# Top-k attention and two MLPs on one core: round one with 256 tokens in two halves, e scaled on GpSimd in the last two rounds, and another order

## The chip, the core and the metric

The kernel runs on one core of one Trainium2 chip. The engines are called by their profile names: PE (TensorE, the matmuls; PEld its weight loads), DVE (VectorE), ACT (ScalarE), POOL (GpSimd) and SP (SyncE, whose queue issues nearly all DMAs). The metric is the device time of one execution in microseconds. Inputs and outputs lie in device memory; working tiles lie in SBUF and matmul results in PSUM.

## What is computed

Attention over 2 batches of 8 heads, 576 positions, head size 64, in which each row keeps its 32 largest scores; its output, 1152 tokens of 512 numbers, goes through two MLPs with a hidden size of 2048.

```python
scores = scale * np.matmul(q, k.transpose(0, 1, 3, 2))
kth = np.partition(scores, -top_k, axis=-1)[..., -top_k:-top_k + 1]   # top_k = 32
scores = np.where(scores >= kth, scores, -1000000000.0)
attn = np.exp(scores - max); attn = attn / (sum + 1e-09)
x = matmul(attn, v) as (1152, 512)
h = x @ w_in;  g = h * np.tanh(softplus(h));  x = g @ w_out        # first MLP (mish)
h = x @ w_in2; g = np.maximum(h, 0) ** 2;     out = g @ w_out2     # second MLP (squared relu)
```

The weights reach the kernel as 64-bit floating-point numbers, seen as pairs of 32-bit words.

## The kernel before

**Rounds.** `ROUNDS` cuts the 1152 tokens into four rounds of 192, 320, 320 and 320 tokens. The code counts them from 0; in this text "round one" is round 0 of the code. While the MLPs of a round run on PE, the attention of the next rounds runs between their matmuls.

**Attention.** A round works through groups of tokens and, for each, four pairs of heads. A *tile* is 128 rows of scores against 576 keys (`tile_of`; a remainder of 64 tokens makes one tile of two heads); all rounds together have 72. A tile's steps: scores on PE into PSUM (line 411); copy to `s` by ACT; the 32nd largest on DVE by four MAX8 (427, 431) and three MATCH_REPLACE8 (430) that write `w`; `nm` on POOL (441); two ACT passes that make `e`; five transposes of `e` on PE (452, 454); copy to `pt` by ACT. `pair_end` waits for all tiles of a pair of heads and multiplies `pt` with the values (497). `inverse` takes the sums of `e`, adds 1e-9 (482, POOL), inverts them (527, DVE), spreads them over partitions with matmuls against the identity (534, 537) and copies them to `inv` by ACT; the product is scaled by `inv` on DVE into `x1` (512).

**MLPs.** Each round has four phases of 64 products of 128x128 weights: `in_phase`, `out_phase`, and both again for the second MLP (all in line 741). Round one uses 32-bit matmuls, two instructions each. The other rounds split weights and activations into a high and a low part and use three matmuls per product. `in_phase` needs `x1` of all four pairs of heads before it gets past its first output tile. Splitting `x` (276), `g` (276, POOL) and squaring (936 POOL, 938 DVE in the last round, `RELU`) lie on the other engines.

**Weights.** The weights are 32 pieces of 128x1024. `convert` makes each into 32-bit numbers in round one: 1 MB read, one ACT pass, one POOL pass (636), one DVE pass (638). Pieces 0 to 23 are then split (`split_w`: high part on ACT, low part in four instructions on POOL, 287) and stored to device memory; the last eight are stored unsplit and split in round two (`fetch_late`). Rounds two to four fetch the split pieces again. A converted piece waits in a place of its own until the phase that uses it releases it: four places used `once` (free parts of `first` and `stage`, and `xl`) and six halves of three shared buffers that come back when their piece has been used.

**Order.** `Order` is a planner: every step is a process that asks for an engine with a cost and a rank; the lowest rank goes first, and the instructions are written to each engine's queue in that order. On the chip each queue runs strictly in this order and waits by semaphores. The numbers at the head (`BUFS`, `CONV_EVERY`, `EARLY`, `STAY`, ...) and the ranks steer it.

## Time and profile before

| | us |
|---|---|
| median of 3 runs | 685.98 (684.62 to 689.83) |
| the profiled execution | 684.57 |
| its span, first to last instruction | 682.8 |

The span is what the views cut into stretches; the profiled execution is 1.8 us longer than its span and 0.2% below the median. Over the span PE is busy for 89%, DVE for 68%, ACT for 59% and POOL for 52%. Such averages hide that the kernel has stages: PE waits in the first hundred microseconds and has the engines nearly to itself in the last two hundred. Matmuls overlap, so that "busy" PE can still run below its rate; the distance between the starts of matmuls tells the rate.

### The profile page before, as it was taken

How to read it: one execution, taken by the hardware profiler on the slowest of the kernel's cores; microseconds unless marked ns; L12 is line 12 of the kernel's file. 1: busy time of each engine (PE TensorE's matmuls, PEld its weight loads, DVE VectorE, ACT ScalarE, POOL GpSimd, SP SyncE). 2: the span in 40 equal slices, each digit the busy share in tenths (PEclk: the TensorE clock that was granted, in tenths of full speed). 3: DMA queues.
4: the chain of work that ended last, by engine and by line, in shares of the span. 5: the costliest groups of instructions: out<-in, count | busy, mean ns of one | idle time of the engine just before them, and what ended most of it. 6: DMA issues, size and time to landing. Idle time of an engine off the chain costs nothing.

```text
span 682.8 us, 11207 instructions
## 1 busy us (share of the span) xinstructions
PE 608.7 (89%) x4104; PEld 559.7 (82%) x4104; DVE 464.1 (68%) x832; ACT 406.0 (59%) x723; POOL 356.2 (52%) x478
## 2 busy tenths in 40 slices
PE   4456569998969799979999999999999999999998
PEld 3334349987767678968889988898999999999997
DVE  5979999999888999988999999997500100001410
ACT  3656568977785567994668877599704404502410
POOL 7998662597996565760238886023207703501420
PEclk9976679999989999999999999999999999999999
DMA  9688851499869989964563379885668899888870
GB/s 345 224 332 311 323 207 75 142 379 381 308 256 369 417 329 394 417 243 148 219 206 111 144 249 347 357 314 198 232 235 304 298 308 325 301 304 304 304 257 29
DMA packets 36598, 186.84 MB, mean 274 GB/s; under 512 B 5312, under 2 KB 11456, under 8 KB 17088
## 3 DMA queue, kind: packets, MB, share of 16 engines
q1 hardware_dynamic: 36272, 185.94, 73.5%
q8 instruction: 32, 0.52, 0.3%
q10 hardware_dynamic: 272, 0.20, 0.1%
q14 instruction: 22, 0.18, 0.1%
HBM read 146.01 MB, written 40.11 MB: 273 GB/s over the span
## 4 chain that ended last, share of the span: by engine, by line
PE 58%; DVE 22%; POOL 11%; ACT 3%; issue 3%; DMA 3%; DVEq 0%; POOLq 0%; ACTq 0%
PE pm L741 48%; DVE w L430 8%; DVE mx L431 7%; POOL w L287 4%; DVE w L638 4%; PE ps L411 3%; PE px L497 3%; DVE mx L427 2%; PE pt L452 2%; POOL stage L636 2%; POOL gl L276 1%; DMA stage<-in_weights 1%; ACT w L270 1%; POOL nm L441 1%; DMA w<-kept 1%
## 5 line engine op out<-in xcount | busy, mean ns | idle before, releaser
L741 PE MATMUL pm<-xh,w 128*128 128x320 f32 (+1 forms) x896 | 200.2, 315 | 5.5 <-ACT xh L270 2.8
L741 PE MATMUL pm<-gh,w 128*128 128x320 f32 x768 | 177.8, 313 | 0.0
L431 DVE MAX8 mx<-w 128x8 f32<-128x576 f32 x216 | 164.4, 761 | 7.4
L741 PEld LDWEIGHTS pm<-xh,w 128*128 128x128 f32 x896 | 152.7, 191 | 7.2 <-ACT xh L270 3.1
L741 PEld LDWEIGHTS pm<-gh,w 128*128 128x128 f32 x768 | 131.0, 189 | 0.7 <-issue 0.3
L741 PE MATMUL pm<-gl,w 128*128 128x320 f32 x384 | 119.7, 312 | 2.2 <-POOL gl L276 2.2
L741 PE MATMUL pm<-xl,w 128*128 128x320 f32 x384 | 119.1, 310 | 0.0
L430 DVE MATCH_REPLACE8 w<-mx,w 128x576 f32<-128x576 f32 x144 | 106.9, 742 | 0.0
L276 POOL TENSOR_TENSOR gl<-h,gh 128x320 fp32r<-128x320 f32 x64 | 56.2, 884 | 85.0 <-ACT gh L270 84.0
L287 POOL TENSOR_TENSOR w<-w,w 128x256 fp32r<-128x256 f32 x112 | 82.8, 763 | 23.3 <-ACT w L270 19.0
L452 PE MATMUL pt<-ident,e 128*128 128x128 f32 x288 | 50.1, 302 | 39.3 <-ACT e L270 36.6
L441 POOL TENSOR_SCALAR nm<-mx 128x1 f32<-128x1 f32 x72 | 31.8, 441 | 85.4 <-DVE mx L431 74.1
L452 PEld LDWEIGHTS pt<-ident,e 128*128 128x128 f32 x288 | 37.6, 153 | 46.4 <-ACT e L270 42.0
L741 PEld LDWEIGHTS pm<-gl,w 128*128 128x128 f32 x384 | 72.8, 190 | 3.0 <-POOL gl L276 2.9
L741 PEld LDWEIGHTS pm<-xl,w 128*128 128x128 f32 x384 | 72.2, 188 | 0.0
L276 DVE TENSOR_TENSOR xl<-pm,xh 128x320 fp32r<-128x320 f32 x12 | 5.9, 488 | 96.8 <-ACT xh L270 96.7
L270 ACT ACTIVATE pt<-pt 128x640 f32<-128x640 f32 x72 | 50.5, 702 | 31.6 <-PE pt L454 31.3
L270 ACT ACTIVATE e<-e,nm 128x576 f32<-128x576 f32 x72 | 55.7, 773 | 19.3 <-POOL nm L441 15.2
L427 DVE MAX8 mx<-s 128x8 f32<-128x576 f32 x72 | 53.5, 743 | 15.9 <-ACT s L270 15.9
L270 ACT ACTIVATE e<-s,mx 128x576 f32<-128x576 f32 x72 | 55.0, 770 | 15.4 <-DVE mx L431 15.2
L430 DVE MATCH_REPLACE8 w<-mx,s 128x576 f32<-128x576 f32 x72 | 53.5, 743 | 0.0
L270 ACT ACTIVATE s<-ps 128x576 f32<-128x576 f32 x72 | 45.8, 636 | 12.2 <-PE ps L411 12.2
(96 smaller groups left out, 988.0 us busy)
## 6 DMA issues: line engine op xcount, KB each, us to landing
w<-both SPq DMA_DIRECT2D x88, 1024.0 KB, 4.9
both<-w SPq DMA_DIRECT2D x32, 1024.0 KB, 6.7
stage<-in_weights SPq DMA_DIRECT2D x22, 1024.0 KB, 7.1
w<-in_weights SPq DMA_DIRECT2D x10, 1024.0 KB, 7.0
vt<-in_v SPq DMA_DIRECT2D x20, 320.0 KB, 4.6
kr<-in_k SPq DMA_DIRECT2D x8, 576.0 KB, 7.6
kept<-w SPq DMA_DIRECT2D x8, 512.0 KB, 11.9
w<-kept SPq DMA_DIRECT2D x8, 512.0 KB, 4.0
```

What stands on the lines that cost most here:

```text
L270: op = ("ACT", t, rank, lambda: nc.scalar.activation(out, in_, func, **kw))
L276: return ({"g": "POOL", "v": "DVE"}[e], t, rank, lambda: eng.tensor_tensor(out=out, in0=in0, in1=in1, op=ALU.subtract))
L287: yield ("POOL", 0.1 + 0.0026 * n, rank, lambda: nc.gpsimd.tensor_tensor(out=out[:, z], in0=in0[:, z], in1=in1[:, z], op=op))
L411: nc.tensor.matmul(sp[:, i, 0:HK], q_, k_[:, i * HK:(i + 1) * HK], start=l == 0, stop=l == len(steps) - 1)
L427: nc.vector.max(out=mx[:, 0, :], in_=s)
L430: nc.vector.match_replace(out=w, in_to_replace=mx[:, i - 1, :], in_values=s if i == 1 else w, imm_value=LOWEST)
L431: nc.vector.max(out=mx[:, i, :], in_=w)
L441: yield ("POOL", 0.38, 1, lambda: nc.gpsimd.tensor_scalar(out=nm, in0=thr, scalar1=mx[:, 0, 0:1], scalar2=scale / UP, op0=ALU.subtract, op ...
L452: nc.tensor.transpose(pp[:, c * P:(c + 1) * P], e[:, c * P:(c + 1) * P], ident)
L497: nc.tensor.matmul(xo[a * D:(a + 1) * D, 0:n], vt[z, a, c, :], pt[z, a, c, 0:n], start=c == 0, stop=c == NK)
L638: yield ("DVE", 1.3, lambda: 15 if x1_done[0].done or i < EARLY else 25, lambda: nc.vector.scalar_tensor_tensor(out=wi, in0=wi, scalar=3, ...
L741: nc.tensor.matmul(o, w[a], x[b], start=first and i == 0, stop=last and i == len(terms) - 1)
```

## The change

- `ROUNDS` becomes 256, 256, 320 and 320 tokens. Round one is two groups of 128 tokens; its first product with `w_in` runs as `half_phase` once for each group, with 128 columns. It takes the pairs of heads as they come (`x0_part`), for three PSUM banks at a time, and holds the eight weight pieces from the first half to the second. Mish is taken over 1024 columns.
- In rounds three and four (`SUMS = "mmpp"`) the sums of `e` are inverted per tile on DVE and `e` is scaled on POOL ahead of its transposes; the spread over partitions, `inv` and the scaling of the product are gone, and DVE copies the product to `x1`.
- In all rounds the attention product runs per tile of 128 rows (`attend`) in place of per pair of heads; `pt` is per tile.
- `COMB`: for pieces 0, 2 and 4 the last step of the conversion is done on POOL by a multiplication by 8 and an addition, in four instructions each. `LO1`: the low parts of the last eight pieces are made on DVE. `XL`: `x` of round two is split on POOL. `RELU`: the squares of round four move to POOL.
- There are five places used once (`x1` and `xh` too, while they are not needed) and other buffer counts: `s` 4, `e` 3, `w` 1, `h` 4, `pt` 2.
- All ranks come from a table, and `CONV_EVERY`, `EARLY`, `SLACK`, `STAY` and `LOOK` change, so that every queue has another order.

The diff, cut to its core:

```diff
-ROUNDS = [[[0, 0, 192]], [[0, 192, 320]], [[0, 512, 64], [1, 0, 256]], [[1, 256, 320]]]
-BUFS = {"s": 3, "e": 2, "w": 2, "kr": 2, "vt": 3, "qr": 2, "kT": 4, "h": 3, "hs": 2, "x1": 2, "pt": 1, "y": 2}
-CONV_EVERY = 2.8
+ROUNDS = [[[0, 0, 128], [0, 128, 128]], [[0, 256, 256]], [[0, 512, 64], [1, 0, 256]], [[1, 256, 320]]]
+BUFS = {"s": 4, "e": 3, "w": 1, "kr": 2, "vt": 3, "qr": 2, "kT": 4, "h": 4, "hs": 2, "x1": 2, "pt": 2, "y": 2}
+CONV_EVERY = 3.5
 EARLY = 12
-BATCHES = [[4, 4, 4, 2, 2]] * 3 + [[]]
-RELU = "pppv"
-XL = " vvv"
-LOOK = 2
+BATCHES = [[4, 4, 4, 4], [4, 4, 4, 4], [4, 4, 4, 4], []]
+RELU = "pppp"
+XL = " gvv"
+SUMS = "mmpp"
+LOOK = 3
...
+LO1 = "v"
+COMB = "gvgvgv"
...
-SLACK = 3.0
-STAY = 7.0
+SLACK = 0.5
...
+STAY = 12.0
...
+        if SUMS[r] == "p":
+            z = acc[:, a:a + 1]
+
+            def invert():
+                nc.vector.tensor_scalar(out=z, in0=z, scalar1=1e-9, scalar2=None, op0=ALU.add)
+                nc.vector.reciprocal(z, z)
+
+            yield ("DVE", 0.25, 3, invert)
+            yield ("POOL", 0.75, RANK["escale"], lambda: nc.gpsimd.tensor_scalar(out=e, in0=e, scalar1=z, scalar2=None, op0=ALU.mult))
...
+    def attend(p, j, unit, pair):
+        n_ = P if j < tiles(group(p)[2])[0] else D
+        for d in unit[2]:
+            yield d
+        yield v_loaded[p]
...
+        def products():
+            for c in range(NK + 1):
+                z = slice(0, P) if c < NK else slice(SR, P)
+                for a in range(2):
+                    nc.tensor.matmul(xo[a * D:(a + 1) * D, j * P:j * P + n_], vt[z, a, c, :], pt[z, a, c, 0:n_], start=c == 0, stop=c == NK)
...
-    late_x = new([P, NC, NMAX], F32, "xl")
-    NG = NF * SIZES[0]
-    once = [x[:, o:o + NW] for x, a in ((first, NG), (stage, 4 * NW), (late_x.rearrange("p c t -> p (c t)"), 0)) for o in range(a, x.shape[1] - NW + 1, NW)]
+    late_x, early_x, free_x = new([P, NC, NMAX], F32, "xl"), new([P, NC, NMAX], F32, "xh"), new([P, NC, NMAX], F32, "x1")
+    sems["x1"].n -= 1
+    N0 = NF * SIZES[0]
+    spots = [(x.rearrange("p c t -> p (c t)"), 0) for x in (free_x, early_x, late_x)] + [(first, N0), (stage, 4 * NW)]
+    once = [x[:, o:o + NW] for x, a in spots for o in range(a, x.shape[1] - NW + 1, NW)]
...
-        yield ("DVE", 1.3, lambda: 15 if x1_done[0].done or i < EARLY else 25, lambda: nc.vector.scalar_tensor_tensor(out=wi, in0=wi, scalar=3, in1=lo, op0=ALU.logical_shift_left, op1=ALU.bitwise_or))
+        if i < len(COMB) and COMB[i] == "g":
+            yield from wide(RANK["cv_g"], ALU.mult, wi, wi, eight.to_broadcast([P, n]))
+            yield from wide(RANK["cv_g"], ALU.add, wi, wi, lo)
+        else:
+            yield ("DVE", 1.3, lambda: RANK["cv_v"] if x1_done[0].done or i < EARLY else 25, lambda: nc.vector.scalar_tensor_tensor(out=wi, in0=wi, scalar=3, in1=lo, op0=ALU.logical_shift_left, op1=ALU.bitwise_or))
...
-        yield from wide(6, ALU.subtract, both[:, 1], w, both[:, 0].bitcast(F32))
+        if lo == "g":
+            yield from wide(RANK["split"], ALU.subtract, both[:, 1], w, both[:, 0].bitcast(F32))
+        else:
+            yield ("DVE", 1.25, RANK["lo1"], lambda: nc.vector.tensor_tensor(out=both[:, 1], in0=w, in1=both[:, 0].bitcast(F32), op=ALU.subtract))
...
+    def half_phase(x, x_done, h, n, held, evict):
+        per = 512 // n * P // FC
+        many = F // FC // per
+        first_banks = 3
+
+        def some(o, k_, cs):
+            for j in range(per):
+                w = held[k_ * per + j][1][0]
+                for i in range(FC // P):
+                    f = j * FC // P + i
+                    for c in cs:
+                        nc.tensor.matmul(o[:, f * n:(f + 1) * n], w[:, c, i * P:(i + 1) * P], x[:, c, h * n:(h + 1) * n], start=c == f == 0, stop=c == NC - 1, skip_group_check=True)
...
+        for c in range(NC - 1):
+            yield x_done[c]
+            for k_ in range(first_banks):
+                yield from piece(k_)
+                yield ("PE", t, RANK["half"], lambda: some(banks[k_], k_, [c]))
+        yield x_done[NC - 1]
+        for k_ in range(first_banks):
+            yield ("PE", t, RANK["half"], lambda: some(banks[k_], k_, [NC - 1]))
+            finish(k_, banks[k_])
+        for k_ in range(first_banks, many):
+            yield from piece(k_)
+            yield sems["ps_m"]
+            o = psum("m")
+            for c in range(NC):
+                yield ("PE", t, RANK["half"], lambda: some(o, k_, [c]))
+            finish(k_, o)
...
+            for h in range(2):
+                yield from half_phase(x1[0], x0_part[h], h, nh, held, lambda k_, o: half_mish(h, k_, o))
```

## Rows read from the trace of the kernel before

**Rows 1.** The page: the chain that ended last, share of the span by engine.

```profile
PE 58%; DVE 22%; POOL 11%; ACT 3%; issue 3%; DMA 3%; DVEq 0%; POOLq 0%; ACTq 0%
```

**Rows 2.** Stretches: length; busy PE, PEld, DVE, ACT, POOL; clock, DMA, GB/s.

```profile
0.00:103.00 103.00, 55.84 (x268) 41.02 (x269) 87.93 (x154) 60.77 (x93) 83.44 (x115) 0.78 0.78 291
103.00:126.00 23.00, 23.00 (x149) 22.89 (x148) 22.24 (x42) 19.58 (x38) 4.40 (x8) 1.00 0.22 74
126.00:251.00 125.00, 109.65 (x688) 96.29 (x687) 115.34 (x189) 91.66 (x152) 100.54 (x130) 0.95 0.86 333
251.00:438.00 187.00, 178.85 (x1331) 163.22 (x1331) 175.01 (x340) 136.10 (x252) 99.31 (x144) 0.99 0.70 260
438.00:683.00 245.00, 241.37 (x1675) 236.28 (x1673) 63.60 (x110) 97.88 (x193) 68.51 (x82) 1.00 0.74 265
```

**Rows 3.** Chain of waits after 490 us: start, us, what.

```profile
497.42 181.97 PE pm L741 x1248
```

**Rows 4.** Timeline of PE around 115 us: start, us, line, operation, count.

```profile
111.45 2.76 PE L741 MATMUL pm<-x,xl 128*128 128x192 f32 x16
114.05 1.46 PE L741 MATMUL pm<-x,w 128*128 128x192 f32 x8
115.35 0.60 PE L452 MATMUL pt<-ident,e 128*128 128x128 f32 x4
115.89 1.47 PE L741 MATMUL pm<-x,w 128*128 128x192 f32 x8
117.06 0.43 PE L411 MATMUL ps<-kT,qs1h 128*128 128x288 f32 x1
117.73 0.49 PE L741 MATMUL pm<-x,w 128*128 128x192 f32 x2
```

**Rows 5.** Timeline of PE around 315 us.

```profile
313.55 2.53 PE L497 MATMUL px<-pt,vt 128*64 128x256 f32 x20
316.00 0.40 PE L411 MATMUL ps<-kT,qs0h 128*128 128x288 f32 x1
...
316.73 0.66 PE L534 MATMUL pt<-ident,acc 128*64 128x128 f32 x8
317.32 0.42 PE L741 MATMUL pm<-gh,w 128*128 128x320 f32 x1
```

**Rows 6.** Groups by line and form, DVE: count, busy, mean ns, idle before.

```profile
L431 DVE MAX8 mx<-w 128x8 f32<-128x576 f32 x216 | 164.4, 761 | 7.4
L430 DVE MATCH_REPLACE8 w<-mx,w 128x576 f32<-128x576 f32 x144 | 106.9, 742 | 0.0
L638 DVE SCALAR_TENSOR_TENSOR w<-w,stage 128x1024 int32<-128x1024 int32 x19 | 25.6, 1354 | 1.6 <-POOL stage L636 1.5
L276 DVE TENSOR_TENSOR xl<-x,xh 128x320 fp32r<-128x320 f32 x12 | 8.8, 766 | 29.5 <-ACT xh L270 29.5
L276 DVE TENSOR_TENSOR xl<-pm,xh 128x320 fp32r<-128x320 f32 x12 | 5.9, 488 | 96.8 <-ACT xh L270 96.7
L527 DVE RECIPROCAL acc<-acc 128x5 f32<-128x5 f32 x8 | 1.4, 177 | 3.2 <-POOL acc L482 3.2
```

**Rows 7.** Groups by line and form, POOL.

```profile
L287 POOL TENSOR_TENSOR w<-w,w 128x256 fp32r<-128x256 f32 x112 | 82.8, 763 | 23.3 <-ACT w L270 19.0 <-issue 2.9 <-POOL w L287 0.4
L636 POOL TENSOR_SCALAR stage<-stage 128x1024 int32<-128x1024 uint32 x22 | 27.2, 1234 | 2.0 <-POOL stage L636 0.3
```

**Rows 8.** DVE timeline: last MAX8 of tile 12, and its pair's scaled product.

```profile
92.69 0.76 DVE L431 MAX8 mx<-w 128x8 f32<-128x576 f32 x1
...
103.00 0.34 DVE L512 TENSOR_TENSOR x<-px,inv 128x192 f32<-128x192 f32 x1
```

**Rows 9.** Line 427: first MAX8 of tiles 16-18 and 32-35.

```profile
L427 DVE MAX8 mx<-s x3: 742/742/754, 110.4 to 122.7; 128x8 f32<-128x576 f32 x3
...
L427 DVE MAX8 mx<-s x4: 742/748/752, 235.9 to 254.7; 128x8 f32<-128x576 f32 x4
```

**Rows 10.** Line 638 alone, one stretch: DVE busy us and conversions.

```profile
126.00:251.00 125.00, 28.46 (x21) 0.95 0.86 333
```

More of the change, by code (lines that the diff above doesn't have):

```diff
@@ L336, in load_v @@
             vt = vts[p] = new([P, 2, NK + 1, D], F32, "vt")
-            yield from sim.dma(lambda: nc.sync.dma_start(out=vt, in_=v[b, pairs[p][2]]), 320, 6)
+            yield from sim.dma(lambda: nc.sync.dma_start(out=vt, in_=v[b, pairs[p][2]]), 320, RANK["load_v"])
             sim.set(v_loaded[p])
@@ L395, in tile_of @@
         acc, _, done = unit[:3]
-        fast = p == 0 and j < 2
+        full = j < nt
+        fast = p == 0 and full
         if p == 0 and not fast:
@@ L539, in inverse @@
         yield ("PE", 0.25 * nt + 0.15 * m, 7, spread)
-        inv = pair["inv"] = sb.tile([P, NMAX], F32, tag="inv", bufs=1, name="inv")
-        yield act(evict_time(n), 9, inv[:, 0:n], pp[:, 0:n])
+        inv = pair["inv"] = sb.tile([P, NG], F32, tag="inv", bufs=1, name="inv")
+        yield act(evict_time(n), RANK["inv"], inv[:, 0:n], pp[:, 0:n])
         give("ps_t")
@@ L546, in topk_attention_two_mlps @@
     x1_part = [[Ev() for _ in range(HP)] for _ in ROUNDS]
+    x0_part = [[Ev() for _ in range(HP)] for _ in ROUNDS[0]]
     def attention():
@@ L673, in put_back, with free_x1 @@
         halves.back(at)
+    def free_x1():
+        yield used[0]
+        give("x1")
     def conversions():
@@ L906, in mish, with half_mish @@
             yield from split_g(i, h)
-        yield from in_phase(x, done, n, mish, r)
         if split_x:
+            yield from in_phase(x, done, n, mish, r)
             give("xhl")
         else:
+            g.append(first[:, 0:NF * n].rearrange("p (f t) -> p f t", f=NF))
+            parts = [Ev() for _ in range(2 * NF)]
+            held, nh = [], n // 2
+            places = {}
+            def half_mish(h, k_, o):
+                b_, at = divmod(k_, 2)
+                if at == 0:
+                    yield sems["hs"]
+                    places[h, b_] = [new([P, 4, NS], F32, "hs").rearrange("p a b -> p (a b)"), 2]
+                while (h, b_) not in places:
+                    yield 0.2
+                hs = places[h, b_]
+                yield act(evict_time(512), RANK["hs"], hs[0][:, at * 512:(at + 1) * 512], o)
+                give("ps_m")
+                hs[1] -= 1
+                if hs[1]:
+                    return
+                m_ = 1024 // nh
+                z = slice(b_ * m_, (b_ + 1) * m_)
+                yield act(0.2 + 0.00085 * 1024, RANK["mish0"], g[0][:, z, h * nh:(h + 1) * nh], hs[0][:, 0:1024].rearrange("p (a b) -> p a b", a=m_), AF.Mish, "mish")
+                give("hs")
+                for k_ in range(z.start, z.stop):
+                    if h:
+                        yield parts[k_]
+                        sim.set(g_done[k_])
+                    else:
+                        sim.set(parts[k_])
+            for h in range(2):
+                yield from half_phase(x1[0], x0_part[h], h, nh, held, lambda k_, o: half_mish(h, k_, o))
             x1_free(0)
@@ L971, in all_mlps @@
             yield from mlps(r)
-    for process in (loads(), load_v(), preparations(), attention(), conversions(), fetches(), all_mlps()):
+    for process in (loads(), load_v(), preparations(), attention(), conversions(), free_x1(), fetches(), all_mlps()):
         sim.spawn(process)
```

211 lines of the change are left out of this document (118 added, 93 removed).

## Prediction

> **What bounds the kernel now.** I read the chain that ended last first, then the busy time in stretches, then single prices. The chain lies 58% on PE and 22% on DVE [rows 1]: the kernel is bound by PE, and before that, in part, by DVE. The stretches show where [rows 2]. I cut them where PE's phases change: to 103 us round one's attention; to 126 its first product with w_in; to 251 its other three phases; to 438 all of round two; then rounds three and four. Up to 103 us DVE is busy for 87.93 us, PE for 55.84 at a granted clock of 0.78, so between 1.2 and 2.4 GHz: PE waits for the top-k of twelve tiles. From 497 us on one piece of 181.97 us with 1248 matmuls closes the chain [rows 3]; there nothing but matmuls counts, 0.1458 us each, 28.0 us for a phase of 192.
>
> Between these two ends the matmuls do not fill PE's time. A 32-bit matmul of 192 columns starts every 2.60 / 16 = 0.1625 us [rows 4], so a phase of round one (128 of them) is 20.8 us. A tile costs PE 0.54 us of transposes and 0.67 us of scores [rows 4], 1.2 in all; a pair of heads with 256 tokens costs 2.45 us for the product with the values and 0.59 us for spreading the inverses [rows 5], with 320 tokens by columns 3.1 and 0.7. So the work after 126 us would be: matmuls 62.4 + 336, some 55 tiles 66 (tile 18 begins at 122.7, [rows 9]), twelve products 37, their spreads 8, and 3.4 us from the end of the last matmul to the end of the span (682.8 - 497.42 - 181.97, [rows 3]): 126 + 513 = 639 us. The span is 682.8. **44 us are waits**, mostly before 438 us.
>
> What PE waits for there is feed. From 126 to 251 us the 21 last pieces of weights are converted [rows 10], 5.95 us each, with DVE busy for 115 of 125 us and POOL for 101 [rows 2]; a piece costs POOL 1.23 us and, if it is split, 4 x 0.763 [rows 7], 4.3 in all. At 103 to 126 us POOL is busy for only 4.40 us and DMA for 22%: all places for converted pieces are full, and PE has not yet used the pieces in them.
>
> **The change, part by part.** *More tokens in round one.* By columns a 32-bit matmul of 128 costs 0.108 us, of 256 0.217, so the first phase is 2 x 13.9 us and each of the other three 27.7. A phase of round two with 256 columns is 22.4 us by columns, 28.0 if nothing shrank; I take 22.4, because 0.1458 us is close to what 320 columns take at 2.4 GHz (0.133). All matmuls: 27.7 x 4 + 22.4 x 4 + 224 = 424 us against 419 before: 5 us more PE work, no gain in itself.
>
> *First product in halves.* The first half needs eight tiles and lies in time in which PE waits now; at 1.2 GHz its 13.9 us would be 27.8, still inside. It costs nothing unless its weights are late, since PE's queue runs in order and the transposes of later tiles stand behind it. The second half has done three quarters of its first three banks when its last pair of heads comes; 12 + 16 products are left, 56 x 0.108 = 6.1 us (12.2 at 1.2 GHz). When is that pair ready? Tile 16 began on DVE at 110.4 us [rows 9]; a tile is 4 x 0.761 + 3 x 0.742 [rows 6], with the short loads between them 5.5 us (12.3 us for two tiles and a conversion, [rows 9]). Three conversions less on DVE are -3 x 1.35 [rows 6]; four more products and inverses +1.4: 113.3. From the last MAX8 of tile 12 (93.5) to its product in x1 (103.3) are 9.8 us [rows 8]. So the phase ends at 113.3 + 9.8 + 6.1 = **129 us**, 3 us later than before, but for 256 tokens in place of 192. This is the gain.
>
> *COMB* puts 24 instructions like line 287 on POOL, 18.3 us, if an integer multiplication is no dearer than the subtraction; at twice that, 37. POOL was busy for 83.4 of 103 us; 102 just fits, 120 does not, and then late pieces cost the second half up to 18 us. I take 18.3: same operands, same width.
>
> *The rest of round one.* PE: 129 + 3 x 27.7 + 16 tiles 19 + four pairs 12 = 243 us. Feed: the eight pieces of the first phase are held to its second half, and five of them lie in places used once, so places come back from about 127 us on; 21 pieces at 4.3 (POOL's own work) to 5.95 us (the pace seen) end at 217 to 252; at the middle, 5.1, at 234, with 3.5 us for the eight products of the last piece. DVE: tile 32 began at 235.9 [rows 9], so it ends at 241.5 - 4.1 + 1.4 = 239 us; 9.8 us later round two has its input. The three limits are 243, 238 and 249: round two starts at **249 us** (251 now).
>
> *Round two.* PE: 249 + 90 + 20 tiles 24 + four products of 320 tokens 12 = 375 us. DVE: 20 tiles 110.8; LO1, eight instructions of the width of line 638, 10.8 us (at worst 8 x 1.9); two one-column instructions a tile for the inverse, 0.177 each [rows 6], 7; splits of x (4 x 0.77 + 4 x 0.49) and four pairs of copies, 8: 137 us after 239, 376. Half of the share that DVE idles now in this stretch (12 of 187 us) adds 4, and the way from the last tile to x1 10 with 0.8 for the scaling of e: round three starts at **390 us** (438 now). Here DVE, not PE, decides; with all of the idle share it is 394, with none and quicker pairs 380.
>
> *Scaling e on POOL* is 40 instructions with one input of 576 columns. Nearest below is line 636, 1.234 us for 1024 [rows 7], so 0.7; above, line 287's two inputs, 0.763 for 256, so 1.7. I take 0.75, as it has one input. POOL is busy for 99 of 187 us in round two, and LO1 takes 24 us from it, so the 30 us fit. What it removes is spread, inv and their waits: 8 us of PE and twelve copies on ACT. What it adds is a wait in the chain of each tile: behind the inverse on DVE the next tile's MAX8 stand, behind the transposes on PE the MLP's matmuls. Three buffers for e in place of two cover it. Squares of round four on POOL (0.95 us each by line 287's columns) and the product per tile (the same columns) I cost at nothing; the cover of the squares is PE's 12 x 0.1458 = 1.75 us per output tile, and without it each of 16 tiles could wait up to 0.95 us. DMA moves the same bytes; its share was at most 0.86 in these stretches.
>
> *Rounds three and four*: 390 + 224 + 20 tiles 24 + four products 12 + 3.4 = 653.5 us. With the 1.8 us around the span (684.57 against 682.8): 655. The runs' median is 0.2% above the profiled execution, which is left out. I round to **654 us**.
>
> **Rivals.** *(a) The waits stay.* Without any wait the changed kernel is 129 + 83 + 90 + 224 + 56 tiles 67 + products and spreads 37 + 3.4 = 633, 635 with the rest. With the 44 us of before it is 679. For it speaks that DVE works 115 of 125 and 175 of 187 us now, and gains only 4 us; against it that PE has 20 us more of matmuls in the stretch that waits for weights, and that DVE has room in the end (63.6 of the last 245 us busy, [rows 2]), so that attention may come later than now. 667 to 684, chance 0.18.
>
> *(b) Two-input instructions of DVE and reads of POOL shut each other out.* The same split of 320 columns takes DVE 766 ns from SBUF and 488 from PSUM [rows 6], so there is such a price. Some 20 two-input instructions of DVE in round two, each held by one whole instruction of POOL (0.75), make 15 us on the engine that decides: round three at 405, 667 us. Chance 0.05, as line 638's mean of 1.354 shows little of it. The Trainium skill has this as a rule ("SBUF — State Buffer", section "Who interferes with whom"): a DVE instruction with two SBUF inputs and a GpSimd instruction that reads SBUF exclude each other, and the second waits for the whole of the first. The two rows agree in sign; by the rule the time is that of (b), by the means the forecast.
>
> *(c) Nearly no waits*: DVE hides its idle share and round three starts at 375: 630 to 641, chance 0.12.
>
> *(d) Slower.* PE's queue is held by e. Each of the 40 scaled tiles passes DVE and POOL between the exponential and its transposes; if POOL is in another instruction then (up to 1.23 us, [rows 7]), the MLP's matmuls stand behind. From 0.8 us a tile on it eats the whole 32 us; at 1.2 us, 48, the time is 702. For it: POOL has 11% of the chain now [rows 1]; against: it is idle for 88 of 187 us in round two [rows 2]. Chance 0.10.
>
> *(e)* No difference, since gains and waits cancel: 0.03.
>
> **How the numbers follow.** The forecast, 641 to 667 us, has 0.52. About 1% can be told from no change, so "same" is 679 to 693. Faster: 0.52 + 0.12 (c) + 0.05 (b) + two thirds of (a) 0.12 = 0.81. Same: the rest of (a) 0.06 + 0.03 = 0.09. Slower 0.10. The range leaves out (d), (e), the upper part of (a) and the lowest of (c), together 0.2: 632 to 680 us.
>
> **What would show it.** Right: round one's first phase ends at 125 to 135 us; the first product of round two starts at 240 to 257 and that of round three at 380 to 396; no spread after round two; the last 150 us are matmuls at 0.146. Wrong: PE waits for conversions (line 638 or its POOL counterpart) after 130 us, which is (a); DVE's two-input rows grow, which is (b); transposes wait long for POOL's e, which is (d); a first half that starts after 60 us, which is a dear COMB.

## The result, and the profile after

The changed kernel takes 675.79 us (median of 4 runs, 675.59 to 678.31) beside 686.15 for the kernel before (4 runs): ratio 0.985, 95% interval 0.980 to 0.990. The forecast was 654 us in a range of 632 to 680. The direction is right and the range holds the time, but of the 32 us expected only 10 came.

The profiled execution, the slowest of the four (678.31 us), has a span of 676.4 us (682.8 before, whose execution of 684.57 us lies below its median). So the two traces differ by 6.4 us where the medians differ by 10.4; what follows accounts for the 6.4. First the stretches, as in [rows 2], cut where tiles 8 and 16 end and where the MLP's phases change; columns: length, busy us of PE, PEld, DVE, ACT, POOL with instruction counts, granted clock, DMA share, GB/s.

```profile
0.00:59.00 59.00, 35.53 (x165) 26.58 (x166) 47.62 (x89) 32.63 (x51) 49.62 (x75) 0.85 0.62 220
59.00:127.00 68.00, 48.64 (x353) 41.95 (x353) 50.58 (x94) 41.91 (x64) 44.67 (x62) 0.75 0.71 269
127.00:148.00 21.00, 15.42 (x105) 13.63 (x103) 16.14 (x31) 11.56 (x17) 9.65 (x15) 0.76 0.51 193
148.00:268.00 120.00, 117.28 (x730) 99.75 (x729) 106.11 (x179) 90.12 (x147) 112.22 (x131) 1.00 0.89 341
268.00:408.00 140.00, 133.59 (x1198) 126.64 (x1197) 126.44 (x261) 98.76 (x183) 94.02 (x102) 1.00 0.83 315
408.00:676.00 268.00, 263.05 (x1948) 256.60 (x1946) 111.95 (x244) 125.92 (x243) 119.69 (x131) 1.00 0.70 253
```

From 148 us on PE is nearly full, at a granted clock of 1.00: 2.7 us idle in 120, 6.4 in 140. Before that it idles 23.5 us of 59, 19.4 of 68 and 5.6 of 21, at 0.75 to 0.85 of the clock. In the stretch 59 to 127 us DVE, which makes the tiles that PE waits for, is itself busy for only 50.58 of 68 us.

The same account for both kernels, cut at 150 us, first the two rows of before, then the two of after:

```profile
0.00:150.00 150.00, 102.84 (x570) 85.70 (x571) 133.66 (x230) 101.71 (x162) 108.59 (x146) 0.85 0.69 258
150.00:663.00 513.00, 489.49 (x3425) 457.89 (x3425) 330.47 (x603) 302.97 (x559) 247.61 (x333) 0.98 0.78 287
```

```profile
0.00:150.00 150.00, 101.58 (x627) 83.94 (x628) 116.27 (x216) 88.05 (x135) 105.64 (x154) 0.80 0.64 237
150.00:663.00 513.00, 501.70 (x3795) 471.28 (x3794) 342.56 (x678) 311.98 (x566) 324.21 (x362) 1.00 0.80 297
```

PE's idle time behind 150 us fell from 23.5 to 11.3 us; ahead of it, it stayed (47.2 and 48.4). Over the whole run PE is busy for 608.7 us before and 613.5 after, so the span moved by -11.2 of idle time and +4.8 of work: -6.4.

The chain that ended last, by engine, beside [rows 1], and its last long piece, beside [rows 3] (start, us, what):

```profile
PE 67%; POOL 12%; DMA 7%; DVE 6%; ACT 5%; issue 2%; SPq 0%; ACTq 0%; POOLq 0%; DVEq 0%
```

```profile
541.90 131.33 PE pm L798 x894
```

DVE's share of the chain went from 22 to 6%. The end is matmuls as before, 131.33 / 894 = 0.1469 us each.

Where the first phase lost its time can be followed in the timelines. The chain's piece on PE first, then POOL, then DVE (start, us, engine, line, operation, count; in brackets the idle time and what ended it). L839 is a matmul of the half phases, L426 the scores, L289 the copy of the next queries, L681 the step of a conversion on POOL, L687 its end on DVE, L456 `nm`, L440 the first MAX8 of a tile and L444 a later one.

```profile
83.94 13.60 PE pm L839 x112
```

```profile
85.70 1.13 POOL L681 TENSOR_SCALAR w<-w 128x1024 int32<-128x1024 uint32 x1
98.01 0.61 POOL L289 CAST qs1h<-qr 128x512 fp32r<-128x512 f32 x1 [11.18 <-PE ps L426]
...
103.90 3.33 POOL L681 TENSOR_SCALAR stage<-stage 128x1024 int32<-128x1024 uint32 x2
107.32 1.32 POOL L456 TENSOR_SCALAR nm<-mx 128x1 f32<-128x1 f32 x1
```

```profile
96.06 0.76 DVE L444 MAX8 mx<-w 128x8 f32<-128x576 f32 x1
105.03 1.23 DVE L687 SCALAR_TENSOR_TENSOR w<-w,stage 128x1024 int32<-128x1024 int32 x1 [8.21 <-POOL stage L681]
107.26 1.23 DVE L687 SCALAR_TENSOR_TENSOR w<-w,stage 128x1024 int32<-128x1024 int32 x1 [1.00 <-POOL stage L681]
108.40 0.76 DVE L440 MAX8 mx<-s 128x8 f32<-128x576 f32 x1
```

112 matmuls of the half phase (two for each product) stand in PE's queue, 13.6 us in one piece, ahead of the last scores that use a buffer of queries (97.3 us). POOL's copy into that buffer waits 11.18 us for them; the conversion behind it on POOL ends late; DVE, at 105.03 next in its order with that conversion, waits 8.21 us; and the next tile's MAX8 stands behind it until 108.40. The first phase ended at 147.9 us (forecast 129).

### The profile page after: what moved, and what is told of

It reads as the page before. It is cut to its first block, busy times and chain, and to the rows that moved or that the text cites. A ratio compares the mean times of both kernels' runs of the same rounds, so it can differ in the third digit from the quotient of the medians.

```text
span 676.4 us, 12051 instructions
## 1 busy us (share of the span) xinstructions
PE 613.5 (91%) x4488; PEld 565.2 (84%) x4488; DVE 458.8 (68%) x893; ACT 400.9 (59%) x702; POOL 429.9 (64%) x515
## 4 chain that ended last, share of the span: by engine, by line
PE 67%; POOL 12%; DMA 7%; DVE 6%; ACT 5%; issue 2%; SPq 0%; ACTq 0%; POOLq 0%; DVEq 0%
PE pm L798 46%; PE px L514 7%; PE ps L426 5%; PE pt L476 4%; PE pm L839 4%; POOL e L469 3%; DMA stage<-in_weights 2%; DVE w L443 2%; ACT e L279 2%; POOL w L296 2%; DVE mx L444 2%; POOL gl L285 2%; POOL h L1064 1%; DMA kept<-w 1%; DMA both<-w 1%
## 5 line engine op out<-in xcount | busy, mean ns | idle before, releaser
L444 DVE MAX8 mx<-w 128x8 f32<-128x576 f32 x216 | 164.4, 761 | 7.4
L798 PE MATMUL pm<-gh,w 128*128 128x320 f32 (+1 forms) x768 | 167.9, 303 | 0.0
L798 PE MATMUL pm<-gl,w 128*128 128x320 f32 (+1 forms) x384 | 115.5, 301 | 0.2 <-POOL gl L285 0.2
L798 PE MATMUL pm<-xl,w 128*128 128x320 f32 (+1 forms) x384 | 115.4, 300 | 0.0
L469 POOL TENSOR_SCALAR e<-e,acc 128x576 f32<-128x576 f32 x40 | 69.5, 1740 | 46.8 <-DVE acc L466 28.5
L285 POOL TENSOR_TENSOR gl<-h,gh 128x320 fp32r<-128x320 f32 (+1 forms) x64 | 54.7, 864 | 40.8 <-ACT gh L279 40.8
L296 POOL TENSOR_TENSOR w<-w,w 128x256 fp32r<-128x256 f32 x76 | 60.3, 814 | 11.0 <-ACT w L279 7.3
L514 PE MATMUL px<-pt,vt 128*64 128x128 f32 (+3 forms) x800 | 62.5, 290 | 1.4 <-ACT pt L279 1.3
L440 DVE MAX8 mx<-s 128x8 f32<-128x576 f32 x72 | 53.7, 746 | 12.2 <-ACT s L279 12.2
L1064 POOL TENSOR_TENSOR h<-h 128x320 f32<-128x320 f32 (+1 forms) x48 | 33.8, 709 | 41.7 <-ACT h L279 41.4
L514 PEld LDWEIGHTS px<-pt,vt 128*64 128x64 f32 (+1 forms) x800 | 45.2, 146 | 17.1 <-issue 11.5
L798 PE MATMUL pm<-first,w 128*128 128x256 f32 x256 | 58.9, 381 | 0.0
```

The source lines that it names most:

```text
L285: return ({"g": "POOL", "v": "DVE"}[e], t, rank, lambda: eng.tensor_tensor(out=out, in0=in0, in1=in1, op=ALU.subtract))
L296: yield ("POOL", 0.1 + 0.0026 * n, rank, lambda: nc.gpsimd.tensor_tensor(out=out[:, z], in0=in0[:, z], in1=in1[:, z], op=op))
L440: nc.vector.max(out=mx[:, 0, :], in_=s)
L444: nc.vector.max(out=mx[:, i, :], in_=w)
L469: yield ("POOL", 0.75, RANK["escale"], lambda: nc.gpsimd.tensor_scalar(out=e, in0=e, scalar1=z, scalar2=None, op0=ALU.mult))
L514: nc.tensor.matmul(xo[a * D:(a + 1) * D, j * P:j * P + n_], vt[z, a, c, :], pt[z, a, c, 0:n_], start=c == 0, stop=c == NK)
```

## Experiments

Ends of phases are the ends of the last matmul into pm, ends of tiles those of the last MAX8 (line 444, 431 before), and a conversion or a round is given by the start of its instruction on DVE or of its first matmul; all are read from the timelines of the profiled executions. Where nothing else is said an edit is made on the changed kernel. Ratios are to the kernel before, run beside it; 0.985 [0.980, 0.990] is the changed kernel's.

| | time, us | ratio [95%] | first phase ends | last conversion on DVE starts | round two starts | round three starts | last tile |
|---|---|---|---|---|---|---|---|
| before | 686.15 | 1 | 125.7 | 241.9 | 251.4 | 438.6 | 486 |
| after | 675.79 | 0.985 | 147.9 | 259.0 | 268.3 | 407.7 | 526 |
| e1_cost | 681.78 | 0.996 [0.993, 0.998] | 134.2 | 262.0 | 275.4 | 411.9 | 509 |
| e5_nocomb | 671.06 | 0.980 [0.978, 0.983] | 140.2 | 255.0 | 261.6 | 401.5 | 515 |
| e11_dve_lo | 694.58 | 1.013 [1.009, 1.018] | 139.7 | 244.2 | 262.1 | 406.4 | 537 |
| e13_two_walls | 673.12 | 0.982 [0.979, 0.985] | 136.1 | 247.5 | 259.5 | 395.7 | 521 |
| e15_sums | 670.91 | 0.980 [0.976, 0.983] | 137.8 | 248.7 | 261.9 | 397.4 | 506 |
| e17_mmmp | 666.76 | 0.973 [0.970, 0.977] | 135.0 | 246.2 | 259.4 | 394.3 | 508 |

### What put 112 matmuls ahead of the scores

The diff itself has the reason. The order is found by a planner that gives each instruction a time; for a step of the half phases that is `mm(n, 3, 0) * per * FC // P`, and since `*` and `//` go from left to right this is 0.225 * 2 * 256 = 115.2 (0.225 us is `mm` for 128 columns), and 115.2 // 128 = 0.0. With the brackets of e1_cost it is 0.225 * 2 * 2 = 0.9 us. In the order half products are free, so any number of them may stand ahead of anything.

e1_cost:

```
-        t = mm(n, 3, 0) * per * FC // P
+        t = mm(n, 3, 0) * per * (FC // P)
```

> The kernel after with one cost of the planner mended: the step of the half products was given mm(n, 3, 0) * per * FC // P, which is 112 // 128 = 0.0 us, and gets 0.22 * 2 * 2 = 0.88 us. The work is the same, only the order of the queues changes. Theory A (the order puts the half products ahead of the scores as if they took nothing, so that scores, POOL's splits behind them and DVE's conversions behind those come late): the first phase of round one ends at 129 to 137 us in place of 147.9, tile 16 at 113 to 119 in place of 127; the time 657 to 666 us. Theory B (POOL is overloaded by COMB and makes the conversions late, in whatever order): the phase still ends at 144 to 150 us, 672 to 680 us. Theory C (the products run at half the clock, whatever their place): a gain of 3 us at most, 671 to 677 us.

The first phase ended at 134.2 us and tile 16 at 115 (127 after), near the forecast's 129 and 113.3; DVE's wait for line 681 in the stretch 59 to 127 us fell from 10.2 to 0.6 us. The two instructions that made POOL wait show the other order (PE's line first): the scores now stand ahead of the half products, and POOL copies the queries at 84.28 us in place of 98.01.

```profile
83.52 0.40 PE L426 MATMUL ps<-kT,qs1h 128*128 128x288 f32 x1 [0.60 <-ACT s L279]
84.28 0.61 POOL L289 CAST qs1h<-qr 128x512 fp32r<-128x512 f32 x1
```

So the zero made the first phase late. But nothing of it came through: round two started at 275.4, later than after, and the time is 681.78 us, slower than after: its interval lies above that of the changed kernel. The trace is of an execution of 678.95 us. The rows from 134 us on, and the two largest waits of PE in the last of these stretches (waiter, releaser, us in total, times, longest):

```profile
134.00:215.00 81.00, 79.89 (x503) 66.70 (x501) 75.11 (x125) 64.41 (x105) 67.21 (x88) 1.00 0.80 297
215.00:275.00 60.00, 48.93 (x312) 39.01 (x313) 47.40 (x88) 32.90 (x57) 53.35 (x52) 0.94 0.91 334
```

```profile
PE pt L476 <- POOL e L469: 4.2, 3, 2.2
PE pm L798 <- DVE w L687: 2.7, 2, 1.6
```

Two phases run full, then PE runs into something: 11 us idle in 60. It waits there for conversions (line 687) and for e scaled on POOL, which begins early because the tiles are early.

e3_both (e1_cost and 1.75 in place of 0.75 as the price of scaling e) and e9_m_cost (e1_cost and SUMS = "mmmm") try whether the scaling is what takes the gain:

```
-            yield ("POOL", 0.75, RANK["escale"], ...
+            yield ("POOL", 1.75, RANK["escale"], ...
```

> As e1_cost, and the planner's cost of scaling e on POOL is 1.75 us in place of 0.75, near the 1.740 us that the instruction took in the kernel after. Same work, another order. Theory D (with the half products counted, the scaled tiles of round three come while the last weights are converted; each holds POOL 1 us longer than planned, so POOL is late with the weights, and what e1_cost gained by 134 us it lost by 275): the first phase ends at 131 to 138 us, round two starts at 255 to 264 us, the time 661 to 669 us. Theory E (the weights set the end of round one: 21 conversions at 5.8 us from the return of the places, whatever the order): round two starts at 268 us or later and the time is 674 to 682 us, as with e1_cost.

> As e1_cost, with SUMS = mmmm: no e is scaled on POOL in any round, and the inverses are spread by PE and multiplied on DVE as before. Theory D: nothing is left that takes POOL longer than planned: first phase at 131 to 138 us, round two from 255 to 264 us, no wait for POOL's e; 660 to 668 us, though PE has 8 us more of spreads. Theory E: round two from 268 us or later, 676 to 686 us.

677.09 us, 0.985 [0.979, 0.992], and 677.42, 0.987 [0.984, 0.991]: the first phase ended at 137.0 and 136.7, the last conversions came at 265.1 and 262.2, round two started at 272.8 and 270.9. The scaling is not what holds round one's end; with or without it the end follows the last conversion by some 8 us. Round one's end stays behind that of the changed kernel in all three runs.

### The parts of the change by themselves

e7_onephase runs the first product as one phase of 256 columns in place of two halves; e8_rounds is the kernel before with ROUNDS of 256 tokens in the first round and nothing else.

```
-            for h in range(2):
-                yield from half_phase(...)
+            yield from in_phase([x1[0]], x1_part[0], n, mish, 0)
```

> The kernel after with the first product of round one in one phase of 256 columns once both groups are there; the rest is unchanged. Theory A: no product stands before the scores of tiles 9 to 16 any more, so tile 16 ends on DVE at 113 to 119 us (127 in the kernel after); the phase has 27.7 us of matmuls after the last pair of heads and ends at 150 to 158 us, the time 676 to 687 us. Theories B and C: tile 16 still ends at 125 us or later, and the phase at 162 us or later, 690 us or more.

> The kernel before with the new ROUNDS alone (256, 256, 320, 320 tokens, round one as one group and one phase), its own order rules and buffers. If the shift of tokens by itself brings the gain: 670 to 678 us. If it does so only where the first product is done in part while PE waits (the view of the forecast): the first phase ends at 150 to 158 us in place of 126, with 27.7 us of matmuls behind tile 16, and rounds two to four save 21 us of matmuls: 688 to 705 us.

698.82 us, 1.020 [1.017, 1.024], and 707.37, 1.033 [1.030, 1.035]: first phase at 162.1 and 154.9, last conversion at 299.5 and 305.7, round two at 309.2 and 311.4. Without half products tile 16 ends at 116 us in e7_onephase, which again puts the late tiles of the changed kernel down to them. More tokens in round one, alone, cost 22 us (685.0 for the kernel before, run beside it): the first phase ends 29 us later, and the conversions, which wait for the places that it holds, end 64 us later (why by so much more was not followed). Against e7_onephase the halves are worth 23 us. In this kernel they are what makes the change pay.

e5_nocomb sets COMB = "", e6_summ SUMS = "mmmm" (no scaling of e on POOL, no inverse for each tile):

> The kernel after with COMB empty: all conversions end on DVE again, POOL loses 24 instructions, some 16 us in the first 90 us, and DVE gets three of 1.3 us. Theory A: POOL was not what held the queue; the first phase still ends at 145 to 152 us and the time is 674 to 681 us. Theory B: the phase ends at 130 to 138 us, the time 660 to 667 us.

> The kernel after with SUMS = mmmm alone (the half products still planned at nothing). If scaling e on POOL costs what PE and its weight loads waited for it in the kernel after (10.1 + 7.8 us, partly the same time) less 8 us of spreads and their waits: first phase unchanged at 146 to 150 us, then 1 to 8 us faster, 668 to 675 us. If those waits are paid by other work that was late anyway: 676 to 684 us.

Without COMB 671.06 us, first phase at 140.2, between the two expectations. The COMB part looks like a loss here, of 3 (by the ratios) to 5 us (by the medians), but the intervals still touch. It has a part in the late first phase, too: without it the first half starts at 34.9 us in place of 43.2, and the phase ends 7.7 us sooner though the zero is still there. Once the zero is mended, COMB no longer moves that end (137.8 and 136.7 us in e15_sums and e16_sums_nocomb below). Without scaling 676.84, 0.985 [0.980, 0.991]: no difference. In this order e scaled on POOL gains nothing.

### What paces the conversions

In each kernel so far round one ended 6 to 13 us behind the last conversion. Three edits, each on one possible cause: AHEAD = 16 (fewer pieces cut and stored in round one), the low half of the odd pieces 9 to 23 cut on DVE in place of POOL, ROLES = "wwwbbb" (a third place for cut pieces, one place less for raw ones).

```
-AHEAD = 24
+AHEAD = 16
```

```
-        yield from split_w(i, both, w, HI[i % len(HI)], RANK["hi0"])
+        yield from split_w(i, both, w, HI[i % len(HI)], RANK["hi0"], "gv"[i % 2] if i >= 8 else "g")
```

> The changed kernel with AHEAD = 16 in place of 24: pieces 16 to 23 are no longer cut into two halves on GpSimd and stored as both (4 quarter subtracts and 1 MB each) during round one; they are stored as one (0.5 MB) and cut in round two, as pieces 24 to 31 were. Theory P (round one ends late because GpSimd and the two places for the halves feed the conversions at 5.8 us a piece): the last 21 pieces come some 12 to 25 us sooner, the last VectorE conversion at 235 to 247 us instead of 259, round one ends at 243 to 256 instead of 268; some of it is paid back in round two, where 8 more pieces are cut on VectorE (1.25 us each) and ScalarE; total 655 to 672. Theory Q (the conversions are paced by the raw loads, the order on SyncE and the transfers, 342 GB/s between 148 and 269 us, and 4 MB less are stored of about 40): last conversion at 250 to 259, total 670 to 680. If round one's end moves with the last conversion in either case, the feed sets it; if the last conversion comes sooner and the end stays at 268, TensorE's own work sets it.

> The changed kernel, but for the odd pieces from 9 to 23 the low half in round one is made by one VectorE subtract (1.26 us) in place of four GpSimd subtracts (3.4 us): 8 pieces, 27 us off GpSimd, 10 us on VectorE, places and transfers as they were. If GpSimd's own time sets the pace of the conversions (it is busy 112 of 121 us between 148 and 269 us): last VectorE conversion 10 to 20 us sooner than 259, round one ends at 250 to 260, total 660 to 670. If the two places and the store behind each set it (about 6 us a place whoever cuts): last conversion within 5 us of 259, total 671 to 680. If VectorE cannot take it (the selection of the top values waits): the tiles 16 to 40 end later than 127 to 300 and the total is 676 to 690.

> The changed kernel with ROLES = wwwbbb in place of wwwbbr: a third place in which a piece is cut and from which it is stored, and one place less for raw pieces (two of three are left). If the two places set the pace (cutting 4 to 5 us and a store of 7.4 us a piece, over two places some 6 us a piece): last VectorE conversion 10 to 25 us sooner than 259, total 655 to 668. If GpSimd's time or the transfers set it: last conversion within 5 us of 259, total 672 to 682. If the raw places set it (load 7 us and conversion 4 us a piece over three places): it comes 10 us or more later and the total is 680 to 700.

e11: the last conversion came at 244.2 us, 15 us sooner, in the middle of what was expected if POOL sets the pace. From 148 to 269 us, after and e11:

```profile
148.00:269.00 121.00, 118.28 (x735) 100.50 (x733) 107.08 (x183) 91.12 (x150) 112.22 (x131) 1.00 0.89 342
```

```profile
148.00:269.00 121.00, 117.85 (x737) 100.78 (x735) 112.37 (x182) 85.17 (x142) 83.36 (x94) 1.00 0.96 364
```

POOL's busy time fell from 112 to 83 us. Round one's end moved by 6 us only (262.1), because PE was full already. e10 takes as much off POOL, and yet its last conversion came only 8 us sooner, at 250.9, where 235 to 247 was expected if POOL sets the pace; round two at 262.1, 698.17 us, 1.019 [1.013, 1.024]. e12: 705.21 us, 1.028 [1.025, 1.032], last conversion at 299.1: with one raw place less they end 40 us later, so these places hold the conversions as well. One more of them was not tried.

In e10 and e11 the time is lost behind round one. From 406 to 424 us, at the start of round three, after and e11:

```profile
406.00:424.00 18.00, 17.04 (x138) 15.79 (x138) 16.37 (x35) 13.37 (x22) 6.03 (x8) 1.00 1.01 421
```

```profile
406.00:424.00 18.00, 10.82 (x65) 8.97 (x65) 15.57 (x37) 8.90 (x17) 8.08 (x9) 0.73 0.76 305
```

PE idles 7.2 of these 18 us in e11 (1.0 after) and does less than half as many matmuls; e10 has 11.65 us of PE there at a clock of 0.72. The last tile ends at 542 and 537 us (526 after), and the end of the kernel comes 155 us behind it (150 after). DVE has 12 us more to do over the run (471 in place of 459), but so it has in e13_two_walls below, which does not lose this time; what empties PE there stays open.

So two things end round one: PE, which from the end of the first phase on takes 116 (e16_sums_nocomb) to 124 us wherever the conversions don't hold it, and the conversions. What paces these is POOL's work in part (e11), and the raw places; the transfers, at a DMA share of 0.96 in e11, have little left. e1_cost shortens the way to the first phase and runs into the second; e11 moves the second and runs into PE. Both together are e13_two_walls:

> Two edits on the changed kernel together: the half products get a price above nothing in the order (0.9 us a step in place of 0.0, the edit of e1_cost), and the low halves of the odd pieces 9 to 23 are cut on VectorE (the edit of e11_dve_lo). Theory W (two things hold the end of round one: TensorE, which from the end of the first phase on needs some 119 to 123 us in every kernel so far, 120.4 after, 121.5 without the sums on GpSimd, 122.6 in e11, 119 in e10; and the conversions, whose last one comes 7 to 13 us before the end, at 262 in e1_cost, where the end came 140 us behind the first phase): with both loosened the first phase ends at 132 to 138, the last conversion comes at 238 to 250, and round one ends at 252 to 260, sooner than with either edit alone (275 and 262). Theory X (something else ends round one at 262 or later whatever these two do, the transfers or the tiles): the end stays at 262 to 275. The total is the end of round one and some 402 to 430 us, since e10 and e11 lost 20 to 25 us behind it, where the tiles of round four are late: 655 to 690.

The first phase ended at 136.1, the last conversion came at 247.5, round two started at 259.5: sooner than with either edit alone, as expected. The time is 673.12 us; on the profiled spans 4.7 us of the 8.8 got through. Its interval still overlaps that of the changed kernel, so this part of the gain is not clear of noise.

e14_reorder: prices of the order set to measured ones and all ranks searched anew. The run changes more than the line shown: CONV_EVERY 2.7, AHEAD 23, SUMS "mmmp", COMB "vgvgvg" and four low halves on DVE.

```
-        return count * (max(0.036, 0.0063 + 0.00044 * n) if r else max(0.075, 0.00057 * n))
+        return count * (max(0.036, 0.0063 + 0.00044 * n) if r else max(0.038, 0.00028 * n))
```

> The changed kernel with the prices of its order set to what the trace measured (half products above nothing, 0.108 us in place of 0.22 for a fp32 product of 128 columns and twice that for 256, the scaling of e 1.75, the conversion on GpSimd 1.38, a quarter subtract 0.83), scaling of e on GpSimd kept for the last round alone, four low halves on VectorE (pieces 13, 15, 23, 25), 23 pieces cut in round one, and the ranks searched anew on these prices. Theory W: the first phase ends at 125 to 135, round one at 248 to 258, and the total comes below both kernels, 645 to 665. If the prices of the order are not what holds it (the waits come from what no price in the list shows, such as GpSimd held by VectorE), the first phase ends at 135 to 148, round one at 258 to 270 and the total is 665 to 685.

693.21 us, 1.012 [1.008, 1.015], a miss: round two started at 287.7. POOL stood 16.6 us in one wait in its new order, 150 to 270 us:

```profile
POOL w L297 <- ACT w L280: 18.4, 3, 16.6
```

This cut (line 297 here) waited for ACT's high half, and every conversion behind it in POOL's queue with it. So better prices were not enough here; whether a rank or one of the other settings does the harm was not tried.

### What keeps the rest

e15_sums is e13_two_walls with SUMS = "mmmm", e17_mmmp with "mmmp" (scaling in the last round alone); e18_nocomb_sums and e16_sums_nocomb take COMB away as well, from e6_summ and from e15_sums.

> e13_two_walls with SUMS = mmmm: no scaling of e on GpSimd and no inverse for each tile on VectorE in rounds three and four; the spread inverse of a pair is multiplied in behind the product, as in rounds one and two. Theory T (VectorE's chain of selections sets the end: last tile and 150 us): 40 times 0.31 us and the waits for the sums, some 12 to 20 us, leave VectorE's chain, the last tile comes at 502 to 512 in place of 521, round one's end stays at 256 to 262, and the total is 655 to 665. Theory N (TensorE's own work sets the end and its idle time is elsewhere): last tile sooner, but the total stays at 670 to 678, since the spread products (13 us in place of 6) come back on TensorE.

> e13_two_walls with SUMS = mmmp: the scaling of e on GpSimd is kept for the last round alone. Half of e15_sums by theory T: last tile at 510 to 517, total 661 to 668; by theory N 670 to 676.

> The changed kernel with COMB empty (no sums of conversions on GpSimd) and SUMS = mmmm: two edits that take work off GpSimd, 9 us in the first 80 us and 70 us behind 254 us, the price of the half products left at 0.0. Theory T: last tile from 515 (e5_nocomb) to 500 to 508, total 658 to 667. Theory N: 668 to 676.

> All four edits: half products priced, odd low halves 9 to 23 on VectorE, no sums on GpSimd, no scaling of e. If the gains add: first phase at 130 to 138, round one at 250 to 258, last tile at 498 to 508, total 650 to 660. If one bound is left for all (TensorE's idle time in the first 150 us, 37 to 47 us in every kernel so far, and some 617 us of its work): 660 to 672.

e15: the last tile ended at 506 us, 15 sooner than in e13 and as expected if DVE's chain of selections set the end, but the time, 670.91 us, fell by 2 us only (the intervals overlap): that theory holds for the tiles and not for the end. The spread products came back on PE, busy for 615.1 us (609.5 in e13). e17: 666.76 us with the last tile at 508. Its interval lies below those of the changed kernel and of e13: it beats both kernels. SUMS = "mmmp" on the changed kernel alone was not tried. e18: 672.97 us, 0.982 [0.979, 0.985]; e16: 668.81, 0.976 [0.973, 0.979], last conversion at 239.9, round two at 252.7. The gains do not add: e16 starts round two 9 us before e15 and ends 2 us sooner.

What DVE stood for before it inverts a tile's sum (line 465), in e13 and in e17, and in e15 what it stands for where the sums of a pair are inverted together (line 567, behind POOL's addition of 1e-9):

```profile
DVE acc L465 <- ACT e L279: 19.4, 13, 5.8
```

```profile
DVE acc L465 <- ACT e L279: 13.0, 8, 5.5
```

```profile
DVE acc L567 <- POOL acc L529: 15.1, 6, 8.8
```

So without any scaling a wait of much the same size stands there for another reason (line 567 waits 2.2 us in e13).

The account of PE at 150 us for e13 and e17:

```profile
0.00:150.00 150.00, 105.43 (x684) 86.20 (x686) 130.65 (x238) 102.79 (x153) 113.22 (x156) 0.87 0.67 250
150.00:663.00 513.00, 498.60 (x3774) 468.42 (x3770) 339.78 (x664) 303.28 (x554) 302.99 (x327) 1.00 0.80 293
```

```profile
0.00:150.00 150.00, 105.38 (x699) 85.96 (x699) 131.26 (x239) 103.97 (x154) 114.57 (x156) 0.90 0.69 252
150.00:663.00 513.00, 503.91 (x3840) 473.81 (x3838) 335.39 (x631) 304.40 (x560) 269.07 (x315) 1.00 0.79 293
```

In e17 PE idles 9.1 of 513 us behind 150 us (14.4 in e13, 11.3 after); 609.3 us of its 663.2 are work. Ahead of 150 us it still idles 44.6 us; in the nine kernels read so it is 41.7 (e1_cost) to 52.0 us (e11_dve_lo). That is what is left, and no run here took it.

## Why the prediction was wrong

By its own steps, in us; the last two columns mend what the runs found.

| step | forecast | after | e13_two_walls | e17_mmmp |
|---|---|---|---|---|
| first phase ends | 129 | 147.9 | 136.1 | 135.0 |
| rest of round one | 120 | 120.4 | 123.4 | 124.4 |
| round two | 141 | 139.4 | 136.2 | 134.9 |
| rounds three and four | 263.5 | 268.7 | 276.0 | 268.9 |
| span | 653.5 | 676.4 | 671.7 | 663.2 |

**The step that failed: the first product "costs nothing unless its weights are late".** The sentence names the right danger, PE's queue in order, and the diff held a reason why it would come true: a price that floors to zero. I read that line as a price. The first phase is 18.9 of the 22.9 us missed. That the zero makes most of it late is shown: with a price it ends at 134.2 us, tile 16 at 115 where 113.3 was forecast (e1_cost). Of the 5.2 us left, 3.5 lie behind tile 16, 19.4 us to the phase's end where 9.8 + 6.1 was taken. Mending this step alone gives no time back, since the next one is wrong as well.

**The feed, 5.1 us a piece, was mis-sized behind it.** After, the 21 conversions from 143.0 to 259.0 us are 20 steps of 5.8 us. It didn't show in the total, since PE was late itself; it shows as soon as PE isn't (e1_cost: 134.1 to 262.0, 6.4 each), and cutting on DVE mends it (e11, e13: 21 conversions between 139.3 and 247.5, 5.4 each). Both ends of the range 4.3 to 5.95 were misread. The pace seen, 5.95, was the stretch of 125 us over 21 pieces; from the first to the last they are (241.9 - 132.3) / 20 = 5.5 us apart. And POOL's 4.3 is only what a piece costs by itself. From 143 to 260 us POOL is busy for 105.07 us, of which the pieces have 43.3 + 20.0 + 7.9:

```profile
L296 POOL TENSOR_TENSOR w<-w,w 128x256 fp32r<-128x256 f32 x52 | 43.3, 852 | 7.7 <-ACT w L279 6.5 <-POOL stage L681 0.5
L681 POOL TENSOR_SCALAR stage<-stage 128x1024 int32<-128x1024 uint32 x14 | 20.0, 1429 | 1.2
L681 POOL TENSOR_SCALAR w<-w 128x1024 int32<-128x1024 uint32 x6 | 7.9, 1324 | 0.5
```

The other 34 us, 1.6 for each piece, are squares, queries, keys and what the tiles need there. The means, 0.852 and 1.3 to 1.4 us, also lie above the 0.763 and 1.234 taken, as VectorE holds POOL up (below).

**"44 us are waits" was half wrong, and [rows 2] had it.** Behind 126 us PE's busy time falls short of the stretches by 15.4, 8.2 and 3.6 us, the last with the 3.4 us of the end in it: 24 us of idle time. The other 20 us were matmuls and transposes dearer than my unit prices when they alternate. The change took 12 of these 24, and e17_mmmp 2 more; the 47 us ahead of 150 us were what was large, and the change took none of them.

**The scaling of e was mis-sized, and its cost is elsewhere.** The forecast took 0.75 us in a range of 0.7 to 1.7:

```profile
L469 POOL TENSOR_SCALAR e<-e,acc 128x576 f32<-128x576 f32 x40 | 69.5, 1740 | 46.8 <-DVE acc L466 28.5 <-ACT s L279 12.7 <-PE pm L798 5.0
```

1.74 us is above the range's top. POOL had the room for 69.5 us; what it costs beside is DVE's queue, where the inverses are 12.3 us of work for all 40 tiles (6.2 for the 20 tiles that the forecast put at 7) and, what the forecast left out, 11 (after) to 19 us (e13) of standing for ACT's sum. Leaving the scaling out of round three alone gives 6 us (e13 against e17). That is shown by the times. That DVE's standing is the way by which it costs fits the tiles (tile 52 ends at 376 us in place of 391), but is argued: in e15, with no scaling at all, DVE stands 15.1 us for POOL's sums instead.

**What held, and what only looks so.** Right were the end (0.1469 us a matmul), no spread behind round two, and the price of COMB's integer multiplications (0.61 us for 256 columns). The first half started at 43.2 us, before the 60 named as a sign of a dear COMB, but without COMB it starts at 34.9 (e5_nocomb), so COMB was not free.

The rest of round one agrees (120 and 120.4) by luck. In the forecast DVE's tiles ended it, at 249, and PE's own sum from 129 to 243 was 114 us; in the trace PE, busy for 117.28 of 120 us, needs the 120. Round two (141 and 139.4) was to be decided by DVE, too, with 126 us for PE. PE is busy there for 133.59 of 140 us, and where DVE's last tile for it comes 12 us sooner (e17, tile 52 at 116.8 us from the round's start in place of 129.0) round two still takes 134.9: the two limits lie so close that the total can't tell them apart. A product of 256 columns took 3.60 / 30 = 0.120 to 3.09 / 24 = 0.129 us in the chain of waits, where 0.117 was taken by columns. The product with the values for each tile, "the same columns" at nothing, is 10 us dearer over the run: it is 800 matmuls in place of 400, and its PE records, each counted until the next one starts, add up to 59.9 us in place of 50.0.

**The rivals.** The time lies in the bounds of (a), the waits stay, but not by its way: the waits it meant, PE's idle time behind 150 us, were halved. That the range of 632 to 680 holds the time is therefore luck: its upper part stood there for (a). (d), the queue of PE held by e, is there with 7.8 us over the whole run, not 32 and more. (b) put the price of shared access on DVE; DVE's rows did not grow (line 687 1.28 and 1.24 us, line 638 before 1.354), and most of the price is POOL's.

## What to carry to other kernels

Where an order is worked out from prices, evaluate each new price by hand: here an instruction priced at zero was put ahead of what the next tile waited for. Bound "waits" by the idle time that the busy column leaves, before a sum of unit prices says more. When a cause found gives nothing back, look for the next one behind it and mend both in one run: here the price of zero and GpSimd's pace hid each other (682 and 695 us alone, 673 together), and with the scaling taken out of round three the three moved 676 to 667 us.

## What the runs showed of the hardware

GpSimd and two-input instructions of VectorE hold each other up, and most of the price lies with GpSimd. In the changed kernel a quarter subtract or sum (line 296, 128x256) takes 0.72 us on average where no conversion or cut of DVE runs (106 of them) and 1.32 where one does (14); line 681 takes 1.14 (25) and 2.12 us (7). In the fences above, line 456, 0.32 us alone, takes 1.32 at 107.32 us, from just behind the start of DVE's 1.23 us at 107.26: the second waits for about 1 us. Where GpSimd's began first, it is DVE's that grows, here to 1.66 us:

```profile
35.42 0.61 POOL L296 TENSOR_TENSOR x<-x,eight 128x256 int32<-128x256 int32 x1
35.46 1.66 DVE L687 SCALAR_TENSOR_TENSOR xh<-xh,stage 128x1024 int32<-128x1024 int32 x1
```

On average DVE's conversions and cuts are 1.31 us with POOL beside them and 1.22 without. The Trainium skill says that a VectorE instruction with two inputs in SBUF contends with a GpSimd instruction that reads SBUF, as by a lock ("SBUF — State Buffer", section "Who interferes with whom"). This trace agrees for lines 296, 456 and 681. It does not for a scaling of e (line 469), which ran beside a cut of DVE for 1.4 us while neither waited for the whole of the other:

```profile
378.41 1.73 POOL L469 TENSOR_SCALAR e<-e,acc 128x576 f32<-128x576 f32 x1
378.73 1.50 DVE L714 TENSOR_TENSOR w<-w,w 128x1024 fp32r<-128x1024 f32 x1 [0.69 <-ACT w L279]
```

An instruction of GpSimd with one input of 128x576 and a scalar of its own for each partition took 1.74 us, 3.0 ns a column, where the conversion's (line 681, two constants) takes 1.14 us for 1024, 1.1 ns.

The granted clock was 0.75, so in part at 1.2 GHz, from 59 to 127 us, where PE was busy for 48.64 of 68 us with waits in between, and 1.00 from 148 us on, where it was busy for 117.28 of 120 us.
